# Attention steps on one core: the products with v moved ahead of the transposes, and one chunk moved to the next unit's first step

## The chip, the core and the metric

The kernel runs on one core of a Trainium2 chip. The metric is the device time of one execution in microseconds (us); lower is better. Before the change the median of three runs is 1220.41 us (1217.64 to 1221.74).

## What is computed

Four batches and eight heads of attention (576 positions, head width 64) with a bias from a small network on relative positions, followed by two feed-forward stages on the 2304 x 512 result. Only the attention matters here:

```python
scores = scale * np.matmul(q, k.transpose(0, 1, 3, 2))
scores = scores + bias.transpose(2, 0, 1)[None, :, :, :]
scores = scores - np.max(scores, axis=-1, keepdims=True)
attn = np.exp(scores)
attn = attn / (np.sum(attn, axis=-1, keepdims=True) + 1e-09)
return np.matmul(attn, v).astype(np.float32)
```

## The kernel before, in words

The program has three stages one after the other: the bias (written to DRAM and read back in tiles), the attention, and the two feed-forward stages. The attention handles 16 units; unit u is one batch of one pair of heads. A unit has five steps p = 0 to 4 (`step`, L417). Steps 0 to 3 each take 128 query rows of both heads; step 4 takes the last 64 rows of both heads together. The order of all work is written out by hand in `step`; each engine runs its instructions in that order, and a unit's late work is done in the next unit's first steps. These are the parts, with the engine that does each:

- `qk` (L303) computes scores on TensorE. Steps 0 to 3 make two score tiles `psS`, one for each head, with tiles of 64 rows by 128 columns of the array (L313), the two heads side by side. Step 4 makes one tile with the whole array (L318). There are two `psS` buffers, so a step's scores wait until VectorE has read those of the step before.
- `softmax` (L321): VectorE adds the bias, writes `e` and takes the extreme value of a row (L327), ScalarE takes the exponential and the sum (L331).
- `tr` (L334) transposes `e` on TensorE with the whole array: nine transposes for a full step (L343, L347), five for the short step (L353, L356). They go through three PSUM buffers with the tag "tr" (named `pt`), which ScalarE and VectorE copy to `eT0` or `eT1` (L344, L348, L354, L357, L358).
- `av` (L360) multiplies chunks of 128 keys of `eT` with v (L370) with tiles of 128 rows by 64 columns, the two heads side by side, and sums over five chunks (c = 0 to 4) in the one buffer `o`. Half 0 covers steps 0 and 1 (256 query columns), half 1 covers steps 2 to 4 (320 columns). A chunk is four matmul instructions.
- `recip` (L376) takes 1/sum on VectorE; `norm` (L382) spreads it over the partitions by TensorE (L389), also with tiles of 128 rows by 64 columns and through a "tr" buffer (named `rp`), and ScalarE copies it to `rbc` (L393).
- `norm_out` (L396): VectorE multiplies `o` by `rbc` to `xt` (L402), which frees `o`; ScalarE and GpSimd split it into two parts (L404, L405).

On TensorE a unit's order is therefore, before the change (the number in brackets counts chunks of products):

```text
step 0: scores, short transposes, products half 0 of u-1 [1: c=4]
step 1: scores, transposes,       products half 1 of u-1 [3: c=0,1,2]
step 2: scores, spread, transposes, products half 1 of u-1 [2: c=3,4]
step 3: scores, transposes,       products half 0 of u   [2: c=0,1]
step 4: scores, spread, transposes, products half 0 of u [2: c=2,3]
```

From unit 4 on, VectorE also converts weights for the later stages between these parts (`w_fill`, L114 to L119, at the end of steps 0 and 3). After unit 15 the tail (L704 to L715) does the short transposes, the last products and the last spread, and starts the feed-forward stage.

Of the kernel before, what the change touches and what calls it, by code (L numbers as in the profile page):

```python
# [7 lines left out]
F32 = mybir.dt.float32  # L8
# [37 lines left out]
def attn_moe(tc, qd, kd, vd, smallp, lrow, ident_d, wf1, wf2, rmsg, out):  # L46
# [3 lines left out]
    def pool(name, bufs=1, space=None, side=None):  # L50
        st = ExitStack()
        kw = {}
        if space is not None:
            kw["space"] = space
        if side is not None:
            kw["side"] = side
        p = st.enter_context(tc.tile_pool(name=name, bufs=bufs, reuse_waits="tile", **kw))
        return p, st
# [105 lines left out]
    def load_k(u):  # L164
        if u < 16:
            hp, b = divmod(u, 4)
            kt = prep.tile([128, 640], F32, tag="k", name="kt", bufs=3)
            nc.sync.dma_start(kt, kd[b, hp])
            kq[u] = [kt, None]
# [10 lines left out]
    def load_bias(hp, j, eng=nc.sync):  # L180
        if hp >= NHP:
            return
        t = prep.tile([128, S], F32, tag=f"bias{j}", name=f"bias{j}", bufs=1)
        if j < 8:
            qt, hh = divmod(j, 2)
            eng.dma_start(
                t, bflat[2 * hp + hh, 128 * qt * ROW:128 * (qt + 1) * ROW]
                .rearrange("(p r) -> p r", r=ROW)[:, 16:16 + S])
        else:

            for p0, c0, c1, k0 in ((0, 0, S, 0), (64, 0, S - 64, 64), (64, S - 64, S, 0)):
                eng.dma_start(
                    t[p0:p0 + 64, c0:c1],
                    bflat[2 * hp + p0 // 64, 512 * ROW:576 * ROW]
                    .rearrange("(p r) -> p r", r=ROW)[:, 16 + k0:16 + k0 + c1 - c0])
        bias_t[j] = t
# [102 lines left out]
    ap, st_ap = pool("att")  # L299

    st = {}

    def qk(u, p):  # L303


        kt, qt_ = kq[u]
        if p < 4:
            pss = [psB.tile([128, 2, 512], F32, tag="S", name="psS", bufs=2) for _ in range(2)]
            for x in range(2):
                for hh in range(2):  # L310
                    r = slice(64 * hh, 64 * hh + 64)
                    k0 = 64 - 64 * hh + 288 * x
                    nc.tensor.matmul(pss[hh][:, x, 0:288], qt_[r, 128 * p:128 * p + 128], kt[r, k0:k0 + 288],  # L313
                                     start=True, stop=True, tile_position=(64 * hh, 0))
            return pss
        ps = psB.tile([128, 2, 512], F32, tag="S", name="psS", bufs=2)
        for x in range(2):
            nc.tensor.matmul(ps[:, x, 0:288], qt_[:, 512:640], kt[:, 64 + 288 * x:352 + 288 * x], start=True, stop=True)  # L318
        return [ps]
# [14 lines left out]
    def tr(u, p):  # L334
        s_ = st[u]
        e = s_["e"].pop(p)
        if p < 4:
            eT, q0 = (s_["eT0"], 128 * p) if p < 2 else (s_["eT1"], 128 * (p - 2))
            for c, ev in ((0, nc.scalar.copy), (2, nc.vector.tensor_copy)):
                pt = psA.tile([128, 512], F32, tag="tr", name="pt", bufs=3)  # L340
                for i in range(4):
                    k0 = 128 * (c + i // 2) + (S + 64) * (i % 2)
                    nc.tensor.transpose(pt[:, 128 * i:128 * i + 128], e[:, k0:k0 + 128], ident)  # L343
                ev(eT[:, 2 * c:2 * c + 4, q0:q0 + 128], pt.rearrange("p (c q) -> p c q", c=4))  # L344

            pt = psA.tile([128, 512], F32, tag="tr", name="pt", bufs=3)
            nc.tensor.transpose(pt[:, 0:128], e[:, 512:640], ident)  # L347
            nc.vector.tensor_copy(eT[:, 8, q0:q0 + 128], pt[:, 0:128])  # L348
        else:
            eT = s_["eT1"]  # L350
            pt = psA.tile([128, 512], F32, tag="tr", name="pt", bufs=3)
            for c in range(4):
                nc.tensor.transpose(pt[:, 128 * c:128 * c + 128], e[:, 128 * c:128 * c + 128], ident)  # L353
            nc.scalar.copy(eT[:, 0:8, 256:320], pt.rearrange("p (c q) -> p c q", c=8))  # L354
            pt = psA.tile([128, 512], F32, tag="tr", name="pt", bufs=3)
            nc.tensor.transpose(pt[:, 0:128], e[:, 512:640], ident)  # L356
            nc.vector.tensor_copy(eT[0:64, 8, 256:320], pt[0:64, 0:64])  # L357
            nc.vector.tensor_copy(eT[64:128, 8, 256:320], pt[64:128, 64:128])  # L358

    def av(u, half, cs):  # L360
        s_ = st[u]
        n = 256 if half == 0 else 320
        eT = s_["eT0"] if half == 0 else s_["eT1"]
        if cs[0] == 0:
            s_["o"] = psA.tile([128, 512], F32, tag="o", name="o", bufs=1)
        o = s_["o"]
        vt = vts[u]
        for c in cs:
            for hh in ((0, 1) if c % 2 else (1, 0)):
                nc.tensor.matmul(o[64 * hh:64 * hh + 64, 0:n], vt[:, c, 64 * hh:64 * hh + 64],  # L370
                                 eT[:, 2 * c + (hh if c < 4 else 0), :], start=(c == 0), stop=(c == 4),
                                 tile_position=(0, 64 * hh))
# [3 lines left out]
    def recip(u, half):  # L376
        s_ = st[u]
        a, z = (0, 4) if half == 0 else (4, 9)
        nc.vector.tensor_scalar(s_["sum"][:, a:z], s_["sum"][:, a:z], 1e-9, None, op0=ALU.add)
        nc.vector.reciprocal(s_["r"][:, a:z], s_["sum"][:, a:z])  # L380

    def norm(u, half):  # L382
        n = 256 if half == 0 else 320
        rp = psA.tile([128, 512], F32, tag="tr", name="rp", bufs=3)
        for qt in range(2 * half, 2 * half + 2 + half):
            for hh in range(2):
                q0 = 128 * (qt - 2 * half)
                c, k0, w = (2 * qt + hh, 0, 128) if qt < 4 else (8, 64 * hh, 64)
                nc.tensor.matmul(rp[64 * hh:64 * hh + 64, q0:q0 + w],  # L389
                                 st[u]["r"][:, c:c + 1].to_broadcast([128, 64]), ident[:, k0:k0 + w],  # L390
                                 start=True, stop=True, tile_position=(0, 64 * hh))
        rbc = ap.tile([128, 320], F32, tag="rbc", name="rbc", bufs=2)
        nc.scalar.copy(rbc[:, 0:n], rp[:, 0:n])  # L393
        st[u]["rbc", half] = rbc
# [12 lines left out]
    def start_unit(u):  # L407
        hp, b = divmod(u, 4)
        vt = ap.tile([128, 5, 128], F32, tag="v", name="v", bufs=2)
        nc.sync.dma_start(vt, vd[b, hp])  # L410
        vts[u] = vt
        sm = ap.tile([128, 32], F32, tag="sm", name="sm", bufs=2)
        st[u] = {
            "m": sm[:, 0:9], "sum": sm[:, 10:19], "r": sm[:, 20:29], "e": {},
        }

    def step(u, p):  # L417
        hp, b = divmod(u, 4)
        if p == 0:
            start_unit(u)  # L420
        if u == 0 and p == 0:
            for j in (6, 7, 8):
                load_bias(0, j)
        if u > 0 and p in (1, 3):
            norm_out(u - 1, p // 2)
        pss = qk(u, p)
        if p == 2 and u > 0:
            norm(u - 1, 1)
        if p == 4:
            norm(u, 0)  # L430
        for j, ps in enumerate(pss, 2 * p):
            softmax(u, j, ps)
            if b == 3:
                load_bias(hp + 1, j)
        if p == 0:
            if u > 0:
                tr(u - 1, 4)
        else:
            if p == 1:
                st[u]["eT0"] = ap.tile([128, 9, 256], F32, tag="eT0", name="eT0", bufs=1)  # L440
            if p == 3:
                st[u]["eT1"] = ap.tile([128, 9, 320], F32, tag="eT1", name="eT1", bufs=1)
            tr(u, p - 1)
        if u > 0:
            if p == 0:
                av(u - 1, 0, [4])
                recip(u - 1, 1)
            if p == 1:
                av(u - 1, 1, [0, 1, 2])
            if p == 2:  # L450
                av(u - 1, 1, [3, 4])
        if p == 2:
            recip(u, 0)
        if p == 3:
            av(u, 0, [0, 1])
        if p == 4:
            av(u, 0, [2, 3])
        if p == 2:
            load_k(u + 2)
            load_q(u + 2)  # L460
        if u >= 4 and p in (0, 3):
            w_fill()
            if p == 3:
                w_tick(lambda i: i < WA)
# [238 lines left out]

    tr(15, 4)  # L704
    recip(15, 1)
    av(15, 0, [4])
    norm(15, 1)
    norm_out(15, 0)
    for i in range(6):
# [84 lines left out]
```

## Time and profile before

| what | value |
|---|---|
| runs | 1217.64, 1220.41, 1221.74 us |
| profiled execution | 1223.03 us |
| its span, first to last instruction | 1221.3 us |
| TensorE clock granted, mean of the span | 0.994 of full |
| first scores of unit 0 | 60.31 us |
| unit 1 begins, tail begins | 79.24 us, 355.11 us |
| busy over the span: matmuls, VectorE, ScalarE, GpSimd | 98%, 68%, 44%, 29% |

The span is what the profile's views divide up; the execution's time lies 1.7 us above it. In the timeline view each row is a run of like instructions with its start and its length; a matmul's end is modelled and overlaps the next one's start, so the time that a block takes on TensorE is read from its start to the start of the next block.

### The profile page before, as it was taken

The numbers are of one execution on the slowest core, as the hardware profiler recorded it, in microseconds if no ns is written. First come the engines' busy times: TensorE is split into PE (matmuls) and PEld (weight loads), VectorE is DVE, ScalarE is ACT, GpSimd is POOL, SyncE is SP. The second block draws the span as 40 slices with busy tenths as digits, with TensorE's granted clock in tenths as the row PEclk, the third lists the DMA queues.
The fourth block names the chain that finished last, engine by engine and source line by source line (L and its number), as shares of the span: only waits on it lengthen the run. The fifth ranks groups of instructions, "written<-read, shape, count | busy, mean of one in ns | idle before, by whom it ended". The sixth has DMA issues, their size and how long they took to land.

```text
span 1221.3 us, 17470 instructions
## 1 busy us (share of the span) xinstructions
PE 1196.8 (98%) x6596; PEld 917.1 (75%) x6596; DVE 836.2 (68%) x1593; ACT 537.8 (44%) x1073; POOL 349.8 (29%) x356
## 2 busy tenths in 40 slices
PE   7899999999999999999999999999999999999998
PEld 2366666666667888888888877878888888888887
DVE  8856667777668988879878989687456255633232
ACT  6856666666655445445435445532232122212111
POOL 4001001101024234224324435674341232124111
PEclk9989999999999999999999999999999999999999
DMA  5932516135001211101110200121011111200012
GB/s 159 293 120 66 177 42 186 58 124 157 23 1 36 70 52 48 56 35 35 56 49 23 64 18 18 41 64 52 18 52 54 33 35 52 70 1 1 35 38 84
DMA packets 30324, 79.26 MB, mean 65 GB/s; under 512 B 3872, under 2 KB 4128, under 8 KB 30240
## 3 DMA queue, kind: packets, MB, share of 16 engines
q1 hardware_dynamic: 29616, 76.09, 19.8%
q0 software_dynamic: 480, 1.77, 0.5%
q8 instruction: 52, 0.85, 0.3%
q14 instruction: 32, 0.26, 0.1%
q10 hardware_dynamic: 144, 0.29, 0.1%
HBM read 62.52 MB, written 15.61 MB: 64 GB/s over the span
## 4 chain that ended last, share of the span: by engine, by line
PE 86%; DVE 9%; ACT 3%; issue 1%; DMA 1%; POOL 0%; DVEq 0%; ACTq 0%
PE y L509 24%; PE h L509 13%; PE hg L509 11%; PE hv L509 11%; PE o L370 7%; PE psS L313 7%; PE pt L343 5%; PE rp L389 2%; DVE ft L248 2%; PE psS L318 2%; PE psb L277 1%; DVE t L548 1%; PE pt L353 1%; DVE r L549 1%; DVE t L547 1%
## 5 line engine op out<-in xcount | busy, mean ns | idle before, releaser
L509 PE MATMUL y<-g,wB 128*128 128x512 f32 (+1 forms) x960 | 214.5, 371 | 5.9 <-DVE yaccs L603 2.2
L509 PEld LDWEIGHTS y<-g,wB 128*128 128x128 f32 x960 | 168.0, 189 | 39.5 <-DVE yaccs L603 3.5
L556 POOL TENSOR_TENSOR g<-t,g 128x512 fp32r<-128x512 f32 (+1 forms) x80 | 97.2, 1215 | 237.4 <-ACT g L555 237.4
L567 POOL TENSOR_TENSOR g<-t,g 128x512 fp32r<-128x512 f32 (+1 forms) x60 | 74.3, 1238 | 292.1 <-ACT g L566 292.1
L327 DVE CUSTOM_DVE_ANT_0 e<-psS,bias 128x576 f32<-128x576 f32 x144 | 103.9, 754 | 74.2 <-PE psS L313 55.0
L509 PE MATMUL h<-xh,wB 128*128 128x512 f32 (+1 forms) x480 | 145.4, 369 | 0.0
L509 PE MATMUL y<-wB,g 128*128 128x512 f32 x594 | 143.6, 389 | 0.0
L331 ACT ACTIVATE e<-e,sm 128x576 f32<-128x576 f32 x144 | 110.6, 769 | 63.5 <-DVE sm L327 63.1
L509 PE MATMUL hv<-xh,wB 128*128 128x512 f32 (+1 forms) x440 | 133.6, 369 | 0.0
L509 PE MATMUL hg<-xh,wB 128*128 128x512 f32 (+1 forms) x440 | 133.1, 368 | 0.4 <-DVE t L562 0.4
L562 DVE TENSOR_TENSOR t<-t,hg 128x512 f32<-128x512 f32 (+1 forms) x60 | 38.0, 633 | 137.4 <-ACT t L561 137.4
L509 PEld LDWEIGHTS y<-wB,g 128*128 128x128 f32 x594 | 110.8, 188 | 22.5
L561 ACT ACTIVATE t<-hg 128x512 f32<-128x512 f32 (+1 forms) x60 | 33.3, 554 | 168.0 <-PE hg L509 161.7
L566 ACT CAST g<-t 128x512 fp32r<-128x512 f32 (+1 forms) x60 | 34.7, 578 | 164.6 <-DVE t L565 164.6
L552 ACT ACTIVATE r<-r 128x512 f32<-128x512 f32 (+1 forms) x80 | 47.1, 589 | 126.0 <-DVE r L549 125.6
L509 PEld LDWEIGHTS h<-xh,wB 128*128 128x128 f32 x480 | 87.8, 188 | 15.9 <-issue 0.5
L370 PE MATMUL o<-eT,v 128*64 128x256 f32 (+1 forms) x640 | 95.0, 418 | 0.0
L509 PEld LDWEIGHTS hg<-xh,wB 128*128 128x128 f32 x440 | 80.5, 188 | 15.0 <-DVE t L562 0.9
L509 PEld LDWEIGHTS hv<-xh,wB 128*128 128x128 f32 x440 | 80.6, 189 | 13.7
L313 PE MATMUL psS<-kt,qt 64*128 64x288 f32 x512 | 89.7, 437 | 0.9 <-DVE sm L327 0.6
L509 PE MATMUL h<-xl,wB 128*128 128x512 f32 (+1 forms) x240 | 88.4, 368 | 0.0
L133 POOL TENSOR_TENSOR wB<-w,wB 128x512 fp32r<-128x512 f32 x58 | 83.1, 1440 | 0.3 <-ACT wB L132 0.3
(116 smaller groups left out, 2119.1 us busy)
## 6 DMA issues: line engine op xcount, KB each, us to landing
raw<-in_wf_dram SPq DMA_DIRECT2D x68, 512.0 KB, 3.6
bflat<-G SPq DMA_DIRECT2D x36, 295.5 KB, 4.1
bias<-bflat SPq DMA_DIRECT2D x26, 288.0 KB, 3.0
kt<-in_kd_dram SPq DMA_DIRECT2D x16, 320.0 KB, 4.6
qt<-in_qd_dram SPq DMA_DIRECT2D x16, 320.0 KB, 4.9
v<-in_vd_dram SPq DMA_DIRECT2D x16, 320.0 KB, 4.4
out_dram<-yacc SPq DMA_DIRECT2D x16, 256.0 KB, 2.1
bias<-bflat POOLq DMA_DIRECT2D x6, 288.0 KB, 5.2
```

What stands on the lines that cost most here:

```text
L133: eng.tensor_tensor(t[:, 1, :], r, t[:, 0, :].bitcast(F32), op=ALU.subtract)
L313: nc.tensor.matmul(pss[hh][:, x, 0:288], qt_[r, 128 * p:128 * p + 128], kt[r, k0:k0 + 288], start=True, stop=True, tile_position=(64 * hh, 0))
L327: nc.vector.tensor_tensor_reduce(out=e.rearrange("p (a b) -> p a b", a=2), in0=ps[:, :, 0:288], in1=bias_t[j].rearrange("p (a b) -> p a b" ...
L331: nc.scalar.activation(e, e, AF.Exp, bias=s_["m"][:, j:j + 1], scale=-1.0, accum_out=s_["sum"][:, j:j + 1])
L343: nc.tensor.transpose(pt[:, 128 * i:128 * i + 128], e[:, k0:k0 + 128], ident)
L370: nc.tensor.matmul(o[64 * hh:64 * hh + 64, 0:n], vt[:, c, 64 * hh:64 * hh + 64], eT[:, 2 * c + (hh if c < 4 else 0), :], start=(c == 0), s ...
L509: nc.tensor.matmul(ps, a, b_, start=(first and k == 0), stop=(last and k == tot - 1))
L552: nc.scalar.activation(r, r, AF.Abs)
L556: nc.gpsimd.tensor_tensor(g[:, 1, :tn], t, g[:, 0, :tn].bitcast(F32), op=ALU.subtract)
L562: nc.vector.tensor_tensor(t, t, pg, op=ALU.mult)
L566: nc.scalar.copy(g[:, 0, :tn], t)
L567: nc.gpsimd.tensor_tensor(g[:, 1, :tn], t, g[:, 0, :tn].bitcast(F32), op=ALU.subtract)
```

## The change

The two chunks of products in step 2 and what stays of those in step 4 are issued straight behind the spread, ahead of the softmax and the transposes of that step. Chunk 3 of half 0 leaves step 4 and joins chunk 4 in step 0 of the next unit (for unit 15 in the tail). Nothing is added or removed: the same instructions run in another order.

```diff
@@ step
         pss = qk(u, p)
         if p == 2 and u > 0:
             norm(u - 1, 1)
+            av(u - 1, 1, [3, 4])
         if p == 4:
             norm(u, 0)
+            av(u, 0, [2])
...
-        if p == 0:
-            if u > 0:
-                tr(u - 1, 4)
-        else:
-            if p == 1:
-                st[u]["eT0"] = ap.tile([128, 9, 256], F32, tag="eT0", name="eT0", bufs=1)
-            if p == 3:
-                st[u]["eT1"] = ap.tile([128, 9, 320], F32, tag="eT1", name="eT1", bufs=1)
+        if p == 1:
+            st[u]["eT0"] = ap.tile([128, 9, 256], F32, tag="eT0", name="eT0", bufs=1)
+        if p == 3:
+            st[u]["eT1"] = ap.tile([128, 9, 320], F32, tag="eT1", name="eT1", bufs=1)
+        if p > 0:
             tr(u, p - 1)
-        if u > 0:
-            if p == 0:
-                av(u - 1, 0, [4])
-                recip(u - 1, 1)
-            if p == 1:
-                av(u - 1, 1, [0, 1, 2])
-            if p == 2:
-                av(u - 1, 1, [3, 4])
+        elif u > 0:
+            tr(u - 1, 4)
+            av(u - 1, 0, [3, 4])
+            recip(u - 1, 1)
+        if p == 1 and u > 0:
+            av(u - 1, 1, [0, 1, 2])
...
-        if p == 4:
-            av(u, 0, [2, 3])
@@ tail
     recip(15, 1)
-    av(15, 0, [4])
+    av(15, 0, [3, 4])
     norm(15, 1)
```

## Rows read from the trace of the kernel before

**Rows 1.** The page's first part: busy time of each engine over the span.

```profile
PE 1196.8 (98%) x6596; PEld 917.1 (75%) x6596; DVE 836.2 (68%) x1593; ACT 537.8 (44%) x1073; POOL 349.8 (29%) x356
```

**Rows 2.** Busy time by stage, units 2 to 15: length, then PE, PEld, DVE, ACT, POOL, granted clock.

```profile
97.64:355.11 257.47, 257.47 (x1921) 162.81 (x1919) 177.51 (x504) 161.01 (x386) 27.01 (x43) 1.00 0.31 96
```

**Rows 3.** Timeline of the matmuls, unit 9: start, length, line, out<-in, count.

```profile
228.23 0.65 PE L370 MATMUL o<-eT,v 128*64 128x256 f32 x4
228.81 1.66 PE L313 MATMUL psS<-kt,qt 64*128 64x288 f32 x8
230.41 1.09 PE L343 MATMUL pt<-ident,e 128*128 128x128 f32 x8
231.34 0.27 PE L347 MATMUL pt<-ident,e 128*128 128x128 f32 x1
231.54 1.83 PE L370 MATMUL o<-eT,v 128*64 128x320 f32 x12
233.31 1.24 PE L313 MATMUL psS<-kt,qt 64*128 64x288 f32 x8
234.48 0.77 PE L389 MATMUL rp<-ident,sm 128*64 128x128 f32 x12
235.18 1.09 PE L343 MATMUL pt<-ident,e 128*128 128x128 f32 x8
...
236.31 1.30 PE L370 MATMUL o<-eT,v 128*64 128x320 f32 x8
237.54 1.24 PE L313 MATMUL psS<-kt,qt 64*128 64x288 f32 x8
...
242.02 0.66 PE L389 MATMUL rp<-ident,sm 128*64 128x128 f32 x8
...
243.74 1.08 PE L370 MATMUL o<-eT,v 128*64 128x256 f32 x8
244.76 0.51 PE L313 MATMUL psS<-kt,qt 64*128 64x288 f32 x2
```

**Rows 4.** Waits of the weight loads, units 1 to 15: us in total, times, longest.

```profile
PEld psS L313 <- DVE sm L327: 5.8, 15, 0.4
```

**Rows 5.** Timeline of VectorE, unit 9.

```profile
229.11 0.08 DVE L327 DVE_READ_ACCUMULATOR2_ANT sm<- 128x1 f32 x1
...
236.31 0.69 DVE L344 COPY eT<-pt 128x512 f32<-128x512 f32 x1 [0.18 <-PE pt L343]
...
237.73 0.49 DVE L402 TENSOR_TENSOR xt<-o,rbc 128x320 f32<-128x320 f32 x1 [0.25 <-ACT eT L344]
238.81 0.76 DVE L327 CUSTOM_DVE_ANT_0 e<-psS,bias 128x576 f32<-128x576 f32 x1 [0.58 <-PE psS L313]
...
242.29 0.75 DVE L327 CUSTOM_DVE_ANT_0 e<-psS,bias 128x576 f32<-128x576 f32 x1
...
244.35 0.28 DVE L348 COPY eT<-pt 128x128 f32<-128x128 f32 x1
```

**Rows 6.** Timeline of the matmuls, unit 0: scores straight behind transposes.

```profile
71.40 0.27 PE L347 MATMUL pt<-ident,e 128*128 128x128 f32 x1
71.60 1.67 PE L313 MATMUL psS<-kt,qt 64*128 64x288 f32 x8
```

**Rows 7.** Timeline of all engines, the tail behind unit 15.

```profile
354.11 0.58 ACT L344 COPY eT<-pt 128x512 f32<-128x512 f32 x1
...
355.11 0.66 PE L353 MATMUL pt<-ident,e 128*128 128x128 f32 x4
...
356.60 0.19 DVE L380 RECIPROCAL sm<-sm 128x5 f32<-128x5 f32 x1
...
356.85 0.77 PE L389 MATMUL rp<-ident,sm 128*64 128x128 f32 x12 [0.39 <-DVE sm L380]
```

**Rows 8.** Groups by line and shape: the products' weight loads, busy, mean ns.

```profile
L370 PEld LDWEIGHTS o<-eT,v 128*64 128x64 f32 x640 | 38.9, 136 | 30.3 <-issue 13.4
```

**Rows 9.** Timeline of ScalarE, unit 9, the copy of step 3's first transposes.

```profile
241.21 0.56 ACT L344 COPY eT<-pt 128x512 f32<-128x512 f32 x1
```

## The prediction

> **What bounds the kernel now.** I read the page's busy times first: the matmuls cover 98% of the span, the next engine 68% [rows 1]. That is an average, so I asked for the stage that the change touches: over units 2 to 15 the matmuls fill 257.47 of 257.47 us, at a granted clock of 1.00, and VectorE 69% of it [rows 2]. A matmul's end is modelled, so "always busy" does not say "always streaming"; the next view, the timeline of one unit, does. I read a block's length from its start to the next block's start, and compare blocks that do the same with different counts [rows 3]:
>
> - Products over 320 columns: three chunks take 231.54 to 233.31 = 1.77 us, two chunks 236.31 to 237.54 = 1.23. One chunk is 0.54, and a block costs 1.23 - 2 x 0.54 = **0.15 more than its chunks**.
> - Products over 256 columns: two chunks take 243.74 to 244.76 = 1.02, one chunk 228.23 to 228.81 = 0.58. One chunk is 0.43 to 0.44, and the block again costs 0.15 more.
> - Scores: 233.31 to 234.48 = 1.17 in step 2, but 228.81 to 230.41 = **1.60 in step 1**, for the same eight matmuls. 0.43 (0.42 to the third digit of most units) is a wait.
>
> So TensorE loses time in two ways: 0.15 per block, each time that the next block uses the array in another shape, and 0.42 in step 1. The list of waits names the second: 15 times, once in each of units 1 to 15, the scores' weight loads end a wait on VectorE's row of the softmax [rows 4]. In unit 9 that is the second head's softmax of step 0, whose last instruction runs 229.11 to 229.19 [rows 5]; it frees the score buffer. Step 0 has too little other TensorE work (the short transposes and one chunk) to cover two softmax instructions.
>
> **The change, part by part.** No instruction is added or removed, no DMA moves, and SP's and GpSimd's order stays.
>
> *Joint of spread and products, steps 2 and 4.* Before: spread, transposes, products, that is three blocks behind the scores. After: spread with products, transposes: two blocks, as spread and products both use tiles of 128 x 64. One surcharge of 0.15 goes. It does so 15 times in step 2 (units 1 to 15) and 16 times in step 4. For the joint itself the trace has no row: nowhere does a product follow a spread. Its cost lies between 0 (as between the chunks of one block) and 0.15 (as at every change of shape) [rows 3]; I take 0, since the chunks of one block are what it is nearest to: same shape, same two column halves. With the joint at 0 the change gains 31 x 0.15 = 4.7 us here, with the joint at 0.15 nothing. The Trainium skill (TensorEngine Tiling (Array Packing), Key Properties) says that changing the tiling mode, not just the tile, drains TensorE; by that rule the joint is free and the sum below stands, and no row shows it. The new neighbours are transposes and scores. Unit 0 shows that pair: from the last transpose to the first scores 71.40 to 71.60 = 0.20 [rows 6], the same as from the last transpose to products, 231.34 to 231.54 [rows 3]. No new cost.
>
> *Chunk 3 of half 0, step 4 to step 0.* It takes 0.43 out of step 4 and puts 0.43 into step 0, ahead of the wait of 0.42. Step 1's scores then arrive at 228.81 + 0.43 = 229.24 in unit 9's time. VectorE is done at 229.19 and its release takes 0.05 to 0.06 (the tail's reciprocal ends at 356.79, the spread that waits for it starts at 356.85 [rows 7]). The wait is gone, just; up to 0.02 may stay. Per unit: -0.43 + 0.43 - 0.42.
>
> *What is late next.* In step 2 the transposes start two chunks later, 235.18 + 1.08 = 236.26, and VectorE's copy with them: 237.39 for 236.31. VectorE keeps its order, so `xt` follows. It stands 1.42 behind that copy, 0.25 of it a wait that goes (the products are now ready) [rows 5]: `xt` at 238.56, at most 238.81, and done 0.49 later, 239.30 at most. Waiting for it: step 3's products, which need `o`. They start 0.15 earlier than before, 239.69: a margin of 0.39 to 0.64. The softmax of step 3 starts at about 238.97, at most 239.22, so up to 0.41 late, and done by 240.0; step 4's scores want its buffer at 242.02 - 0.15 - 1.17 = 240.70. In step 3 the weight conversion follows, then step 4's softmax at up to 242.29 + 0.41 = 242.70, done at about 243.5; the next unit's scores, which want its buffer, now come at 244.76 - 0.15 - 0.15 - 0.43 = 244.03. In step 4 the transposes start one chunk later in a step that begins 0.15 earlier, 0.43 - 0.15 = 0.28, and VectorE's copies behind them end at 244.35 + 0.28 + 0.28 = 244.91. The next unit's softmax starts 1.27 behind its scores (as 238.81 behind 237.54), at 245.30: a margin of 0.39. So all of it fits under TensorE's work, and that cover is gone from a further delay of 0.39 on. `e`, `eT` and `rbc` are written a step or more ahead of their readers.
>
> *The tail.* Unit 15's chunk lands in the tail, where the last spread waits for the reciprocal (356.60 to 356.79). Counted from the start of step 4, the tail's transposes would start 0.43 + 0.15 = 0.58 earlier, at 354.53, but they need a PSUM buffer that ScalarE's copy leaves at 354.69, behind an exponential that keeps its place [rows 7]. With a release of 0.05 they start at 354.74 for 355.11, 0.37 earlier, and the reciprocal and the spread with them; the extra chunk fits into the spread's old wait. So unit 15's step 4 and the tail give 0.37 together. What follows hangs on that spread and shifts along.
>
> **The sum**: 15 x (0.42 + 0.15 + 0.15) + 0.37 = 11.2, less up to 15 x 0.01 of wait that stays: **11.0 us**. Against the profiled execution, 1223.03 us (1.7 above its span), that is 1212.0. The profiled execution is 2.6 above the median of the runs shown, so against the median I predict 1220.41 - 11.0 = **1209.4 us**.
>
> **Rivals.**
>
> *The joint is not free.* The products' first weights might not load beside the spread. A load takes 0.136 [rows 8], close to the surcharge of 0.15. Then 31 x 0.15 = 4.7 come back: 1214.1. The Trainium skill (TensorE: Matmul & The Clock Gate, Part 3, The mechanism) says that weight loads overlap matmuls only where the row group differs; spread and products use the same rows. The trace speaks against it: inside a block, with the rows the same, a chunk's time goes with its columns alone, 0.54 / 0.43 = 1.25 = 320 / 256 [rows 3], which leaves nothing for loads in series. 8 in 100.
>
> *A PSUM buffer comes late.* The spread of step 4 takes one of the three "tr" buffers of step 3; the profile does not show which. If it is the one that ScalarE copies (241.21 to 241.77 [rows 9]), that copy follows the softmax, 0.16 to 0.41 late, so is released at 241.98 to 242.23, while the spread would come at 242.02 - 0.15 = 241.87 [rows 3]. That is 0.11 to 0.36 in 15 units; I price it at 0.11, since the 0.25 is a wait whose cause goes: 1209.4 + 1.7 = 1211.1 (at most 1214.8). 8 in 100.
>
> *The change does not do what it says in step 1.* If step 0's softmax starts 0.42 later than before, because VectorE is still at the copies of step 4, the wait stays whole behind the new chunk, and only the joints count: 15 x 0.30 + 0.4 = 4.9, 1215.5. For: those copies move towards it. Against: the margin of 0.39. 5 in 100.
>
> *Slower.* The same place, further: the two copies of step 4 (0.69 + 0.28 = 0.97) fall wholly ahead of the two softmax instructions of step 0. Step 1's wait is then 0.42 + 0.97 - 0.43 = 0.96 behind the chunk, so a unit changes by 0.96 - 0.42 - 0.30 = +0.24, 15 units by +3.6, less 0.4: 1223.6. The sign turns when the softmax is 0.72 late. Against: the copies would have to come 0.39 + 0.97 later than I work out [rows 5], and VectorE has 31% free [rows 2]. 3 in 100.
>
> **How the numbers follow.** My forecast has 74 in 100, the rivals 8, 8, 5 and 3; 2 are left for what I have not seen. About 0.3% (3.7 us, from 1216.7 on) is what a measurement of this kernel can tell from no change. Forecast, first and second rival lie below it; so does the third, but only by 1.2, and I give it half. Faster 0.92, same 0.05, slower 0.03. The runs shown spread by 2.8 below and 1.3 above their median, so the range goes from 1206.5 up to 1214.3, which takes in the first two rivals.
>
> **What would show it.** In the timeline the scores of step 1 last 1.17, not 1.60, and the wait on L327 is gone from the list; a unit takes 17.7 for 257.47 / 14 = 18.39; spread and products of step 2 together take 1.78 for 0.70 + 1.23 = 1.93; step 3's softmax starts later relative to its scores without any wait of TensorE behind it. Wrong would be: the same 1.93 (the joint costs), a new wait ahead of L389 in step 4 (a buffer), or a wait of L313 in step 1 (softmax late).

## The result and the profile after

The changed kernel takes 1207.59 us (median of 4 runs, 1206.18 to 1209.12) where the kernel before takes 1219.63 (4 runs, 1217.64 to 1221.74): ratio 0.9901, 95% interval 0.9878 to 0.9924. That is 12.0 us less; 11.0 was predicted, 1209.4 for the median, inside the range that was stated. The profiled execution takes 1208.49 us with a span of 1206.7.

The timeline of the matmuls of the changed kernel, unit 9 from step 1 on (start, length, line, out<-in, count), to be read beside [rows 3]:

```profile
221.27 1.24 PE L313 MATMUL psS<-kt,qt 64*128 64x288 f32 x8
222.44 1.09 PE L343 MATMUL pt<-ident,e 128*128 128x128 f32 x8
...
226.51 0.77 PE L389 MATMUL rp<-ident,sm 128*64 128x128 f32 x12
227.11 1.25 PE L370 MATMUL o<-eT,v 128*64 128x320 f32 x8
228.29 1.09 PE L343 MATMUL pt<-ident,e 128*128 128x128 f32 x8
...
229.43 1.24 PE L313 MATMUL psS<-kt,qt 64*128 64x288 f32 x8
...
231.73 1.08 PE L370 MATMUL o<-eT,v 128*64 128x256 f32 x8
...
233.91 0.66 PE L389 MATMUL rp<-ident,sm 128*64 128x128 f32 x8
234.40 0.60 PE L370 MATMUL o<-eT,v 128*64 128x256 f32 x4
234.93 1.09 PE L343 MATMUL pt<-ident,e 128*128 128x128 f32 x8
...
238.94 1.24 PE L313 MATMUL psS<-kt,qt 64*128 64x288 f32 x8
```

Read from start to start: step 1's scores take 222.44 - 221.27 = 1.17 for 1.60. Spread and two chunks in step 2 take 226.51 to 228.29 = 1.78 for 1.93. Spread and one chunk in step 4 take 233.91 to 234.93 = 1.02 for 0.59 + 0.58 = 1.17. From one step 1 to the next, 221.27 to 238.94, a unit takes 17.67, for 18.39 before.

VectorE of the same unit, to be read beside [rows 5]:

```profile
229.43 0.69 DVE L344 COPY eT<-pt 128x512 f32<-128x512 f32 x1 [1.26 <-PE pt L343]
...
230.52 0.46 DVE L402 TENSOR_TENSOR xt<-o,rbc 128x320 f32<-128x320 f32 x1
230.90 0.75 DVE L327 CUSTOM_DVE_ANT_0 e<-psS,bias 128x576 f32<-128x576 f32 x1
...
238.80 0.08 DVE L327 DVE_READ_ACCUMULATOR2_ANT sm<- 128x1 f32 x1
```

The copy now waits for the moved transposes, `xt` stands 1.09 behind it (1.42 before), ends at 230.98 and leaves step 3's products at 231.73 a margin of 0.75. The softmax of step 3 starts 1.47 behind its scores (1.27 before). The last row is the softmax that frees the score buffer for step 1: it ends at 238.88, the scores start at 238.94, 0.06 later, which is the release alone.

Now by stage, from unit 1's short transposes to the tail's. The busy times by stage of the kernel before (length, then PE, PEld, DVE, ACT, POOL, granted clock, DMA):

```profile
80.41:355.11 274.70, 274.70 (x2050) 173.76 (x2048) 189.22 (x538) 172.10 (x413) 28.84 (x46) 1.00 0.30 93
```

and of the changed kernel, the last row being the tail up to the first feed-forward matmul:

```profile
78.20:342.30 264.10, 263.95 (x2049) 167.93 (x2048) 186.15 (x537) 172.20 (x413) 28.85 (x46) 1.00 0.31 97
342.30:344.89 2.59, 2.59 (x25) 1.68 (x25) 1.90 (x7) 0.59 (x1) 0.00 (x0) 1.00 0.00 0
```

The stage gives 274.70 - 264.10 = 10.60. The tail is 0.15 longer (2.44 before), and unit 0's step 4, ahead of the stage, gives the same 0.58 as every step 4 (0.43 + 0.15). Together 10.60 + 0.58 - 0.15 = **11.0 us, the sum that was predicted**. The spans differ by 14.6. In the profile of before TensorE's clock was granted at half for a while in unit 0 and once more at the start of the second feed-forward part. Unit 0 takes 20.10 us there from its first scores to the stage, and 16.44 after: 3.1 more than the change's 0.58. The feed-forward part gives another 1.9. Against this, the bias stage, which the change does not touch, took 1.45 longer in the profile of the changed kernel (first scores at 61.76 for 60.31); both profiles have the clock at half for 3.4 us in that stage. These rows are the stretch before the fall in the feed-forward part and the fall itself:

```profile
688.00:691.80 3.80, 2.25 (x17) 1.86 (x15) 3.77 (x6) 2.01 (x5) 2.00 (x2) 1.00 0.24 47
691.80:695.20 3.40, 3.40 (x17) 3.22 (x17) 2.97 (x8) 1.14 (x3) 0.00 (x0) 0.50 0.26 104
```

The same place of the changed kernel in its profile:

```profile
674.00:678.00 4.00, 2.67 (x19) 2.31 (x18) 3.93 (x6) 2.35 (x6) 2.45 (x2) 1.00 0.01 4
678.00:681.00 3.00, 2.78 (x19) 2.42 (x20) 2.93 (x8) 1.29 (x3) 0.74 (x1) 1.00 0.58 175
```

In both the matmuls pause (busy 2.25 of 3.80 and 2.67 of 4.00 us); before, the clock then stood at 0.50 (1.2 GHz) for 3.4 us, after, it stayed at 1.00 (2.4 GHz). The feed-forward part is 1.9 us shorter for it. Whether that belongs to the change is asked below.

### The profile page after: what moved, and what is told of

It is laid out like the page before. It is cut to its first block, busy times and chain, and to the rows that moved or that the text cites. A ratio compares the mean times of both kernels' runs of the same rounds, so it can differ in the third digit from the quotient of the medians.

```text
span 1206.7 us, 17433 instructions
## 1 busy us (share of the span) xinstructions
PE 1181.8 (98%) x6596; PEld 907.8 (75%) x6596; DVE 832.5 (69%) x1593; ACT 537.9 (45%) x1073; POOL 350.2 (29%) x356
## 4 chain that ended last, share of the span: by engine, by line
PE 84%; DVE 10%; ACT 3%; issue 1%; DMA 1%; POOL 0%; DVEq 0%; ACTq 0%
PE y L506 24%; PE h L506 13%; PE hg L506 11%; PE hv L506 11%; PE o L370 7%; PE psS L313 6%; PE pt L343 5%; PE rp L389 2%; DVE ft L248 2%; PE psS L318 2%; PE psb L277 2%; DVE t L545 1%; DVE yacc L600 1%; PE pt L353 1%; DVE r L546 1%
## 5 line engine op out<-in xcount | busy, mean ns | idle before, releaser
L327 DVE CUSTOM_DVE_ANT_0 e<-psS,bias 128x576 f32<-128x576 f32 x144 | 103.7, 754 | 46.5 <-PE psS L313 31.4
L563 ACT CAST g<-t 128x512 fp32r<-128x512 f32 (+1 forms) x60 | 34.7, 578 | 164.6 <-DVE t L562 164.6
L552 ACT CAST g<-t 128x512 fp32r<-128x512 f32 (+1 forms) x80 | 46.2, 578 | 81.3 <-DVE t L551 76.7
```

The costliest lines, as they stand in the source:

```text
L327: nc.vector.tensor_tensor_reduce(out=e.rearrange("p (a b) -> p a b", a=2), in0=ps[:, :, 0:288], in1=bias_t[j].rearrange("p (a b) -> p a b" ...
L552: nc.scalar.copy(g[:, 0, :tn], t)
```

## The experiments

**The joints alone.** From the changed kernel, chunk 3 goes back to step 4:

```diff
-            av(u, 0, [2])
+            av(u, 0, [2, 3])
...
-            av(u - 1, 0, [3, 4])
+            av(u - 1, 0, [4])
...
-    av(15, 0, [3, 4])
+    av(15, 0, [4])
```

> The joints alone: in steps 2 and 4 the products stand behind the spread, but chunk 3 of half 0 stays in step 4. Theory (a change of array shape costs 0.15 us, a joint of the same shape nothing; step 1's wait of 0.42 is a matter of its own): 31 x 0.15 = 4.7 us below the kernel before, about 1215; the scores of step 1 still take 1.59 to 1.60 us; spread and two chunks in step 4 take 0.49 + 0.97. Rival 1 (the gain comes from the chunk alone, the order inside a step costs nothing): no change. Rival 2 (products early in a step are what ends step 1's wait, since the transposes' copies move): the scores of step 1 fall to 1.17 and the time by 11.

1214.91 us (8 runs; before beside it 1218.98, 13 runs), ratio 0.9971 (0.9953 to 0.9990). Timeline of the matmuls, step 4 of unit 5 and step 1 of unit 6:

```profile
165.00 0.66 PE L389 MATMUL rp<-ident,sm 128*64 128x128 f32 x8
165.48 1.03 PE L370 MATMUL o<-eT,v 128*64 128x256 f32 x8
166.45 1.09 PE L343 MATMUL pt<-ident,e 128*128 128x128 f32 x8
...
170.03 1.66 PE L313 MATMUL psS<-kt,qt 64*128 64x288 f32 x8
171.62 0.33 PE L343 MATMUL pt<-ident,e 128*128 128x128 f32 x1
```

Spread and two chunks take 0.48 + 0.97, the scores of step 1 still 1.59. The stage (same ends as above) takes 270.41, 4.29 less than before: 30 joints at 0.15 make 4.5, and the last unit gives back 0.2, where the tail's short transposes wait for ScalarE's copy. Both rivals fall: the order inside a step is worth its 0.15, and step 1's wait does not care for it.

**The chunk alone.** From the kernel before:

```diff
-                av(u - 1, 0, [4])
+                av(u - 1, 0, [3, 4])
...
-            av(u, 0, [2, 3])
+            av(u, 0, [2])
...
-    av(15, 0, [4])
+    av(15, 0, [3, 4])
```

> The chunk alone: the order inside steps 2 and 4 as before, chunk 3 of half 0 moves from step 4 to step 0. Theory: the chunk's 0.43 us fills the wait of 0.42 in step 1, so 15 x 0.42 = 6.3 us below the kernel before, about 1213.5; scores of step 1 at 1.17, the joints' blocks as before (spread 0.59 and 0.70, products 0.58 in step 4). The two single parts add up to the whole change (4.7 + 6.3 = 11.0). Rival (the parts help each other): less than 4 us here, or the two together far from 11.

1212.25 us (6 runs, same runs of before), ratio 0.9948 (0.9930 to 0.9966). Timeline of the matmuls, step 1 of unit 6:

```profile
169.36 1.24 PE L313 MATMUL psS<-kt,qt 64*128 64x288 f32 x8
170.53 0.33 PE L343 MATMUL pt<-ident,e 128*128 128x128 f32 x1
```

1.17: the wait is gone. The stage takes 268.43, 6.27 less. The two parts add up in the stage: 4.29 + 6.27 = 10.56, where the whole change gives 10.60. They do not help each other.

**A second chunk to step 0.**

```diff
             norm(u, 0)
-            av(u, 0, [2])
...
-            av(u - 1, 0, [3, 4])
+            av(u - 1, 0, [2, 3, 4])
...
-    av(15, 0, [3, 4])
+    av(15, 0, [2, 3, 4])
```

> From the changed kernel, chunk 2 goes to step 0 as well, so step 4 has no products. Theory: the wait of step 1 is already filled, so the second chunk is only moved: step 4 loses 0.43 us, step 0 gains 0.43, the number of shape changes is the same: within 1 us of the changed kernel, 1207 to 1209. Rival (any product moved into step 0 runs free, since step 0 is short): another 6 us less, about 1201.

1206.40 us (6 runs), ratio to before 0.9907 (0.9888 to 0.9926), as the changed kernel's 0.9901. A unit takes 17.67 as in the changed kernel. The stage takes 264.53, 0.43 more, all of it behind unit 15, whose last transposes, the tail's short ones and ScalarE's copy are:

```profile
338.64 1.09 PE L343 MATMUL pt<-ident,e 128*128 128x128 f32 x8
...
339.79 0.57 ACT L344 COPY eT<-pt 128x512 f32<-128x512 f32 x1
...
340.42 0.66 PE L353 MATMUL pt<-ident,e 128*128 128x128 f32 x4 [0.58 <-ACT eT L344]
```

The transposes of step 4 last 340.42 - 338.64 = 1.78 for 1.35 in the changed kernel: the short ones wait for a buffer that ScalarE's copy leaves at 340.36, so taking chunk 2 out of step 4 gains nothing there. The gain of the move was the wait that it filled, and one chunk fills it.

**Transposes first.** The pair of spread and products goes behind the transposes:

```diff
-        if p == 2 and u > 0:
-            norm(u - 1, 1)
-            av(u - 1, 1, [3, 4])
-        if p == 4:
-            norm(u, 0)
-            av(u, 0, [2])
...
             tr(u, p - 1)
+            if p == 2 and u > 0:
+                norm(u - 1, 1)
+                av(u - 1, 1, [3, 4])
+            if p == 4:
+                norm(u, 0)
+                av(u, 0, [2])
```

> From the changed kernel, steps 2 and 4 do the transposes first and then the spread with the products behind it, joined as in the change. Theory (the number of shape changes counts, not that the products are early): the same number of changes of shape, so within 1 us of the changed kernel, 1207 to 1209. Rival (it counts that products come ahead of the transposes, which then wait less for exponentials or buffers): the joints' 4.7 us are lost, about 1212.

**1235.12 us** (5 runs), ratio to before 1.0132 (1.0115 to 1.0150): slower than both kernels, and neither theory said so. The expectation also miscounted: in step 4 scores and transposes, both with the whole array, now stand side by side, one change of shape fewer. Timeline of the matmuls, a step 2:

```profile
239.08 1.09 PE L343 MATMUL pt<-ident,e 128*128 128x128 f32 x8
240.01 0.27 PE L347 MATMUL pt<-ident,e 128*128 128x128 f32 x1
241.39 0.77 PE L389 MATMUL rp<-ident,sm 128*64 128x128 f32 x12 [1.11 <-DVE eT L344]
242.00 1.25 PE L370 MATMUL o<-eT,v 128*64 128x320 f32 x8
```

VectorE in the same step:

```profile
239.29 0.76 DVE L327 CUSTOM_DVE_ANT_0 e<-psS,bias 128x576 f32<-128x576 f32 x1 [1.45 <-PE psS L313]
...
239.98 0.75 DVE L327 CUSTOM_DVE_ANT_0 e<-psS,bias 128x576 f32<-128x576 f32 x1
...
240.65 0.69 DVE L344 COPY eT<-pt 128x512 f32<-128x512 f32 x1
```

And its list of waits of the weight loads:

```profile
PEld rp L389 <- DVE eT L344: 32.9, 29, 1.3
```

In a step 2 the spread should follow the last transpose by 0.20, at 240.21, and starts at 241.39, 1.18 late. It needs one of three "tr" buffers, and the transposes of its own step have just filled all three. VectorE empties the one that it gets only behind two softmax instructions, 240.65 to 241.34, and the spread starts 0.05 later. In step 4, with one softmax, it is 0.74 late (scores and transposes joined take 1.08 free of waits, the transposes' block 1.82 here). In the stage that makes 15 x 1.18 + 15 x (0.74 - 0.15) = 26.6, and it took 290.46 - 264.10 = 26.4 more. So the shape is not all: the spread belongs ahead of its step's transposes, where its buffer is one of the step before. My second rival had the right resource, in a place where it does not bind.

**Spread and chunk 2 at the end of step 3.**

```diff
-        if p == 4:
-            norm(u, 0)
-            av(u, 0, [2])
...
             av(u, 0, [0, 1])
+            norm(u, 0)
+            av(u, 0, [2])
```

> From the changed kernel, the spread of half 0 and chunk 2 go from step 4 to the end of step 3, behind the products there: one block of spread and products fewer, and step 4's scores and transposes, both with the whole array, become one block. Theory of shapes alone: two surcharges of 0.15 less in 16 units, 4.8 us below the changed kernel, about 1203. Theory of shapes and buffers: the spread now stands behind all three transposes' tiles of its own step and waits for VectorE's copy of one, which stands behind two softmax instructions (in the changed kernel it ends at 232.94, the spread would come at 232.65): 0.3 to 0.4 per unit come back, so 1207 to 1209, with a wait of L389 on L344 in the list.

1211.08 us (6 runs; before 1218.98, 11 runs), ratio 0.9935 (0.9921 to 0.9948), slower than the changed kernel (1206.81 on the same chip). Timeline of the matmuls, steps 3 and 4:

```profile
215.24 1.08 PE L370 MATMUL o<-eT,v 128*64 128x256 f32 x8
216.50 0.66 PE L389 MATMUL rp<-ident,sm 128*64 128x128 f32 x8 [0.18 <-DVE eT L344]
216.98 0.60 PE L370 MATMUL o<-eT,v 128*64 128x256 f32 x4
217.52 1.24 PE L318 MATMUL psS<-kt,qt 128*128 128x288 f32 x4
218.59 1.04 PE L343 MATMUL pt<-ident,e 128*128 128x128 f32 x8
```

Two chunks without a change of shape behind them should need about 0.91 (1.01, less the 0.10 that a spread saves in step 2 when products follow it, 0.60 for 0.70); they take 216.50 - 215.24 = 1.26, so some 0.35 is the buffer's wait, as foretold, again on L344. The scores of step 4 take 1.07 for 1.17 and the transposes behind them 1.07 for 1.13: their change of shape is gone. With the 0.10 behind the products, shapes give some 0.25 and the buffer takes 0.35, so a unit takes 17.77 for 17.67. The median lies 2 above what I expected and 4.3 above the changed kernel. The stage is 2.1 longer (266.22): 0.10 in each unit, and 0.8 behind the last, where unit 15's short transposes come too soon and wait for the last exponential (the transposes ahead of them last 1.98). The rest goes with the clock: the profile has it at half for some 6 us in unit 0, and the one run at a mean clock of 1.000 took 1209.03.

**Spread early in step 3.** It takes a buffer of the step before:

```diff
+        if p == 2:
+            recip(u, 0)
+        if p == 3:
+            norm(u, 0)
-        if p == 4:
-            norm(u, 0)
-            av(u, 0, [2])
...
-        if p == 2:
-            recip(u, 0)
         if p == 3:
-            av(u, 0, [0, 1])
+            av(u, 0, [0, 1, 2])
```

> From the changed kernel, the spread of half 0 goes to step 3 ahead of its transposes (1/sum is taken at the start of step 2 for that), chunk 2 joins chunks 0 and 1 behind the transposes of step 3, step 4 keeps scores and transposes alone. Theory of shapes and buffers: the spread takes a buffer of the step before, which is free; scores and transposes of step 4 are one block, so one surcharge of 0.15 less in 16 units, 2.4 us; behind step 4's scores only the transposes (1.1 us) are left to cover its softmax, so the next unit's second scores wait some 0.1 in 15 units. Together 1206 to 1208, at most 2.4 below the changed kernel. Theory of shapes without buffers: the same 2.4 and no more than e5 gives.

1206.87 us (4 runs), ratio to before 0.9899 (0.9887 to 0.9912); the changed kernel on the same chip 1206.81. Timeline of the matmuls, step 4:

```profile
195.62 1.24 PE L318 MATMUL psS<-kt,qt 128*128 128x288 f32 x4
196.69 1.04 PE L343 MATMUL pt<-ident,e 128*128 128x128 f32 x8
...
197.77 0.51 PE L313 MATMUL psS<-kt,qt 64*128 64x288 f32 x2
```

No wait for a buffer, scores and transposes as one block (1.07 + 1.08), and a unit at 17.52 for 17.67. The wait of 0.1 that I expected behind step 4 came in unit 1 alone, whose scores of step 1 take 1.55 for 1.17:

```profile
77.63 1.62 PE L313 MATMUL psS<-kt,qt 64*128 64x288 f32 x8
79.18 0.33 PE L343 MATMUL pt<-ident,e 128*128 128x128 f32 x1
```

The stage takes 262.92, 1.2 less; the tail's wait for the last exponential keeps 0.9. The same with unit 15 in the old order, from the kernel with the spread early:

```diff
-        if p == 3:
+        if p == (3 if u < 15 else 4):
             norm(u, 0)
+        if p == 4 and u == 15:
+            av(u, 0, [2])
...
-            av(u, 0, [0, 1, 2])
+            av(u, 0, [0, 1, 2] if u < 15 else [0, 1])
```

> As the run with the spread early in step 3, but unit 15 keeps the changed kernel's order, since in that run the tail's transposes waited for the last exponential (their block of step 4 lasted 1.99 us for 1.08) and gave back 0.9. Theory: 14 or 15 units at 17.52 us for 17.67, so 2.2 us below the changed kernel at the same clock, 1204 to 1205, and a tail of the changed kernel's length. Rival: the gain is lost elsewhere in any case, 1206 to 1207.

1206.73 us (4 runs), ratio 0.9902 (0.9888 to 0.9917), with the changed kernel beside it 1207.24 (5 runs), 0.9912 (0.9897 to 0.9927):

> The changed kernel beside it on the same chip, for the comparison: 1206 to 1208, about 11 below the kernel before where the clock is the same.

The stage takes 262.38, 1.7 less (14 units at 0.15, less a single wait of 0.38 in unit 1), but the median is above the 1204 to 1205 that I expected, and the intervals overlap. It beats the changed kernel in the stage's trace; that it does so in time is not shown.

**One change of shape more.** From the changed kernel, chunk 4 of half 1 goes behind the transposes:

```diff
-            av(u - 1, 1, [3, 4])
+            av(u - 1, 1, [3])
...
             tr(u, p - 1)
+            if p == 2 and u > 0:
+                av(u - 1, 1, [4])
```

> From the changed kernel, chunk 4 of half 1 goes behind the transposes of step 2, chunk 3 stays behind the spread: one more change of shape in 15 units, and nothing else moves. Theory: 15 x 0.15 = 2.3 us above the changed kernel, about 1210; the two product blocks take 0.64 and 0.69 for one of 1.18. Rival (what counts is only that no block of products starts cold behind transposes with its operands just written): no change.

1210.82 us (6 runs; the changed kernel on the same chip 1206.81), ratio to before 0.9931 (0.9919 to 0.9944). Timeline of the matmuls, step 2:

```profile
207.69 0.71 PE L370 MATMUL o<-eT,v 128*64 128x320 f32 x4
208.33 1.09 PE L343 MATMUL pt<-ident,e 128*128 128x128 f32 x8
...
209.46 0.76 PE L370 MATMUL o<-eT,v 128*64 128x320 f32 x4
210.15 0.51 PE L313 MATMUL psS<-kt,qt 64*128 64x288 f32 x2
```

0.64 + 0.69 = 1.33 for 1.18, and the rival (no change) falls: one more change of shape costs the same 0.15, and the stage is 266.35 - 264.10 = 2.25 = 15 x 0.15 longer.

**The changed kernel again.**

> The changed kernel once more, for its time and for the clock: in the profile of before TensorE's clock was at half for 6.8 us in unit 0 and for 3.4 us at 692 us, in the profile of after at neither place. If that belongs to the change, this profile shows neither again; if it differs from run to run, one may be here.

1206.81 us (4 runs), ratio 0.9901 (0.9888 to 0.9914); its stage takes 264.10, as in the first profile. Its profile and that of the third set show the clock at half at neither place. But other variants that touch nothing in the feed-forward part have the fall there: the one with the split products (3.4 us at 680), the two with the spread early (at 676), the one with the transposes first (at 704). So that fall is not tied to the change. The fall in unit 0 stands in the profiles of before, of the joints alone, of the chunk alone and of the spread at the end of step 3, and in no other. It begins at about 63 us, in unit 0's first steps, ahead of the first instruction that any of these orders moves; with one profile of most kernels, whether it is rarer after the change is open. Over all runs whose mean granted clock is 1.000, before averages 1217.3 us (14 of 33 runs) and the changed kernel 1206.6 (8 of 13 runs): 10.7 us.

## Why the prediction was right

*What bounds the kernel* held: blocks measured from start to start gave both costs, 0.15 per change of shape and 0.42 in step 1, and each was confirmed by itself (4.29 us of the stage, with 0.2 more lost in the tail, and 6.27).

*The joint*, for which the trace of before had no row, costs nothing: 1.78 for 1.93 and 1.02 for 1.17. The first rival, that the products' weights load only behind the spread, falls with it. Two further orders show that it is the shape that counts: products split by transposes pay 0.15 more, whole-array scores with transposes behind them 0.15 less. The Trainium skill (TensorEngine Tiling (Array Packing), Key Properties) says that a change of the tiling mode, and not of the tile alone, drains TensorE; these runs agree with it.

*The chunk* filled the wait exactly, with the 0.06 of the release and nothing over: step 1's scores take 1.17 to 1.18 in all 15 units.

*What is late next* held too: the margins were worked out at 0.39 to 0.64 for `xt` and came to 0.75, since the smaller instructions between the copy and `xt` closed up further than I took. The spread of step 4 follows its scores after 1.17 in every unit, so the second rival's buffer was free in time.

*The tail* was mis-sized: 0.37 predicted from step 4 to the first feed-forward matmul, 0.22 measured (6.35 to 6.13). The timeline of the changed kernel's tail:

```profile
340.95 1.09 PE L343 MATMUL pt<-ident,e 128*128 128x128 f32 x8
...
342.08 0.69 DVE L344 COPY eT<-pt 128x512 f32<-128x512 f32 x1 [1.28 <-PE pt L343]
342.30 0.42 PEld L353 LDWEIGHTS pt<-ident,e 128*128 128x128 f32 x4 [0.38 <-ACT eT L344]
...
342.89 0.14 PEld L356 LDWEIGHTS pt<-ident,e 128*128 128x128 f32 x1 [0.17 <-issue]
```

The first short transposes start 3.54 after step 4's scores (338.76), as worked out (354.74 - 351.20). The last one then comes 0.62 behind them, for 0.49 before (355.11 to 355.60), and the reciprocal and the last spread follow it. Its row puts the pause to "issue"; by the order of the buffers it needs the one that VectorE's copy, 342.08 to 342.77, leaves, and the prediction had looked at ScalarE's copy alone. Here luck came in: the sum had taken off 0.15 for a wait that might stay in step 1 and did not, and the tail gave 0.15 less than I had counted. The two cancel, so the agreement of 11.0 with 11.0 is closer than its terms.

*One reading was wrong without harm to the sum.* I took the list's row on L327 [rows 4] for step 1's wait and said that it would go. The list of the changed kernel still has it:

```profile
PEld psS L313 <- DVE sm L327: 5.8, 15, 0.4
```

Its 0.4 is a pause that the weight loader makes at changes of shape where nothing is waited for as well (0.39, put to "issue", ahead of the spread in the changed kernel), put down here to the semaphore that came last. The wait itself stood inside the block, between the first and the second head, and shows only in the block's length.

The rest of the 12.0 us, some 1 us beyond the sum, is within the interval. The two later sets give 12.2 and 11.7 by their medians, and at the same clock the two kernels lie 10.7 apart; so what is beyond the sum goes with the clock, which the sum left out, and whether the change has a part in that is not shown.

## What to carry to other kernels

When one engine is always busy by the profile, measure its blocks from start to start and compare blocks of the same work with different counts: the constant that is left is the price of a change, and the odd one out holds a wait. Put work of the same array shape side by side, but look first from which step its buffer comes: the same pair behind the transposes cost 26 us of the stage. Moving work into a wait pays the length of the wait and no more; here a fit with nothing to spare held in every unit.

## What the runs showed that I had not expected

Whole-array scores and transposes count as one shape: the scores' block falls from 1.17 to 1.07 and the transposes' from 1.13 to 1.08 where they touch. And TensorE's clock fell to half for 3.4 us, at a pause of the matmuls that every variant has at the start of the second feed-forward part, in some executions and not in others; each such fall there makes the feed-forward part some 2 us longer (863.7 to 864.1 us for 861.8 to 862.0), which is a sixth of what this change is worth.
